# Attention and two MLPs on one core: layer 2 in two channel halves, weight checks by a second reading, one predicated copy a step

## The chip, the cores and the metric

The kernel runs on one NeuronCore of a Trainium2 chip. The time is the device time of one execution in microseconds (us); three runs were taken. [...]

## What is computed

Three layers in a row, all in float32. First attention with 2 batches, 8 heads, 768 positions and 64 channels a head, in which a query sees the 128 positions up to its own and the first few positions of the sequence (sinks). Then two MLPs on the 1536 tokens of 512 channels, each through 2048 hidden channels:

```
scores = where(is_sink | in_window, scale * q @ k.T, -1e9)
a = softmax(scores);  x = (a @ v), heads side by side      # 1536 x 512
h = x @ w_in1;  g = (a0 + a1 h + a2 h^2 + a3 h^3) / (1 + |b0||h| + |b1| h^2 + 1e-6);  x = g @ w_out1
h = max(x @ w_in2, 0);  out = (h * h) @ w_out2
```

The weights lie in memory as 8-byte words. The kernel turns them into float32 by integer operations on the two halves of each word, and a check that no weight is too small for that way is part of the program: a flag at the end of the kernel sends unusual inputs to a slow general path, which does not run here.

## The kernel before

**Precision.** Every matmul operand is split into a high and a low part (`xh`, `xl`; `gh`, `gl`; the two rows of a weight tile `w`), and three products are made of them, so each 128 x 128 x 512 block of a product costs three matmuls.

**Attention.** A block `u` is 128 queries of all heads; there are 12 blocks, six a batch, and each takes four steps `n` (two heads a step). In step `n` the program gives out, engine by engine and in the order of the code: ACT's exponentials of step `n-1` (`expo`, L371), PE's scores of step `n` into two PSUM banks `s` (L341), DVE's predicated copy and masked minimum of them (`s` L349, `ns` L354), PE's transposes of step `n-2` (L394), ACT's copies of the sink columns into `sk` (L383), POOL's two selects that make `ph` out of `pc` (L403, L407), PE's products with the values (`O` L431), and, once a block, the transpose of `sk` (L414), the products with the sinks' values (L438, L440), the scaling `x` (L443) and its transposes and split (L296, L212, L213). Queries and keys of the next block are split by ACT and POOL (`ql`, `kl`, L303). There are four banks `s`, so the scores of a step wait until DVE has read those of two steps before. PE also runs filler matmuls of zeros (L467), up to eight a step in the first twelve steps, three a step in the first block of a batch, and twelve at the end.

**Weights.** There are 64 weight tiles of 512 KB, 32 a layer. `w_load` has four of them on the way (tile `wr`). `w_step` takes a tile in four DVE instructions: a minimum of absolute values `wmin` (L164), then three integer operations (L171, L178, L183) that make the float32 tile `wx`. `w_fin` splits it by ACT and POOL into `w`. `w_until(due(k))` says how many of these instructions must have been given out by slot `k`: 13 tiles during attention, the other 19 of layer 1 until slot 30, ten of layer 2 until the end of layer 1, and the last 22 at two tiles a slot from there. In attention the function `extra` gives them out after each step but those with `n % 4 == 2`.

**Layers.** A slot `k` is one pass of 128 hidden channels `f` for a chunk `c` of 512 tokens: first the products with `w_in` into a bank `T` (function `g1`, 12 matmuls, L536), two slots later those with `w_out` into four banks `s` (`g2`, 12 matmuls, L612). In between lie the activation on ACT, DVE and POOL. Layer 1 has 48 slots: two halves `g` of the hidden channels, in each the three chunks, in each eight `f`. At the end of a chunk `finish` takes the four banks to SBUF: in the first half copies `part` (DVE L638 two, ACT L640 two), in the second half sums with them (DVE L635). Layer 2 has 48 slots too: three chunks of 16 `f`, and `finish` copies to `o` (DVE L644, ACT L646), from where SP sends it out. A bank `T` is free for `g1` of two slots on when DVE has read it for the last time (L577 in layer 1, L570 in layer 2), and PE waits for that. In slot `k` the order of the code is: split of the activation two slots back, `w_fin` twice, DVE's activation of `k-1` with `finish` ahead of it, `g1(k+1)`, ACT's activation of `k`, weight steps, `g2(k-2)`.

`verdict` makes the flag at slot 68, with one small matmul on PE and a reduction on DVE that waits for it.

Of the kernel before, what the change touches and what calls it, by code (L numbers as in the profile page):

```python
# [15 lines left out]
P = 128  # L16
# [3 lines left out]
WS = 4  # L20
# [6 lines left out]
LEAST = 2.0 ** -15 * 1.125  # L27


@with_exitstack  # L30
def kernel(
# [52 lines left out]
    hsum = cst.tile([P, NCH * NF], F32, name="hsum")  # L84

    wmin = cst.tile([P, 4 * NF], F32, name="wmin")

# [51 lines left out]
    parts = {}  # L139

    def w_load():
        m = wst["load"]
        if m >= len(wtiles):
            return
        wst["load"] += 1
        L, f, j = wtiles[m]
        src = ((w_in1, w_out1), (w_in2, w_out2))[L][j].bitcast(I32)
        r = wr.tile([P, DM, 2], I32, tag="wr", name="wr", bufs=NWR)
        if j == 0:
            nc.sync.dma_start(  # L150
                out=r.rearrange("p (c f) t -> p c (f t)", c=KD),
                in_=src[:, 2 * f * P:2 * (f + 1) * P].rearrange("(c p) f -> p c f", p=P),
            )
        else:
            nc.sync.dma_start(out=r.rearrange("p n t -> p (n t)"), in_=src[f * P:(f + 1) * P, :])
        wraw[m] = r

    def w_step():
        m, i = divmod(wst["int"], WS)
        wst["int"] += 1  # L160
        r = wraw[m]
        low, high = r[:, :, 0], r[:, :, 1]
        if i == 0:
            nc.vector.tensor_reduce(  # L164
                out=wmin[:, m:m + 1], in_=high.bitcast(F32), axis=AX.X, op=ALU.min, apply_absolute_value=True
            )
            return
        if i == 1:
# [6 lines left out]
            return  # L175
        x = wt[m]
        if i == 2:
# [3 lines left out]
        else:  # L181
            y = wx[m] = wr.tile([P, DM], I32, tag="wx", name="wx", bufs=2) if conv["psum"] else x
# [3 lines left out]
            del wraw[m], wt[m]  # L186
            w_load()

    def w_until(steps):
        while wst["int"] < min(steps, WS * len(wtiles)):  # L190
            if wst["int"] % WS == (WS - 1 if conv["psum"] else 1) and len(wx) == 2:
# [28 lines left out]
    def ps_s():  # L220
        return ps.tile([P, 512], F32, tag="S", name="s", bufs=4)
# [11 lines left out]
    def attention(ap, extra, ahead):  # L233
# [6 lines left out]
        ld, qs, vs, pr_t, pT, kps, ops, sk, sT, rs_t = {}, {}, {}, {}, {}, {}, {}, {}, {}, {}  # L240
# [90 lines left out]
        def scores(n):  # L331
# [3 lines left out]
            d = [ps_s() for _ in range(2)]  # L335
# [11 lines left out]

# [657 lines left out]
```

## Time and profile before

| | |
|---|---|
| three runs | 716.63, 718.15 (median), 720.15 us |
| span of the profiled execution, first to last instruction | 716.1 us |
| attention, until the first matmul of layer 1 | 152.7 us |
| matmuls of the two layers, to the last one's end | 557.4 us |
| PE busy | 689.8 us, 96% of the span |
| DVE, ACT, POOL busy | 447.8, 376.4, 355.7 us |
| TensorE's mean granted clock | 0.949 |

The profiler's span leaves out what lies around the program; the runs stand 0.5 to 4.1 us above it. PE's busy time is that of overlapping matmuls whose ends are modelled, so 96% says that PE is the engine to look at and not that nothing can be gained on it: what matters is at which clock it ran, and where it stood still.

### The profile page before, as it was taken

Reading aid. Unit: us, or ns where it says so; the run is one execution under the profiler, and the core shown is the slowest. Engines: PE = TensorE matmul, PEld = TensorE weight load, DVE = VectorE, ACT = ScalarE, POOL = GpSimd, SP = SyncE. Lnnn points to the kernel's source line nnn. Section 1 sums busy time; section 2 is a strip of 40 time slices with the busy share of each in tenths; the row PEclk is TensorE's granted clock in tenths of the full one; section 3 lists DMA queues with packets and bytes.
Section 4 is the critical chain, followed back from the end, with each engine's and each line's share of the span. In section 5 each row is a group of like instructions: output and inputs, shape, how many; then the busy total and the mean of one; then the engine's idle time right before and its main releaser. Section 6 shows DMA issues by size and latency. Waiting matters only on the chain.

```text
span 716.1 us, 9442 instructions
## 1 busy us (share of the span) xinstructions
PE 689.8 (96%) x3210; PEld 554.7 (77%) x3210; DVE 447.8 (63%) x942; ACT 376.4 (53%) x851; POOL 355.7 (50%) x341
## 2 busy tenths in 40 slices
PE   9999899997999999999999999899999999999996
PEld 6778788886877878878778788677787788878885
DVE  4899865548979979799797894999602211021111
ACT  4688654446868868778598692433322222222221
POOL 3788555324655646656486583776522222222221
PEclk9999755589999999999999999999999999999999
DMA  8556522101111212112021120555001000010001
GB/s 222 148 138 161 148 74 59 60 30 29 60 59 60 88 39 80 59 59 59 30 62 57 46 72 1 175 176 176 3 1 59 1 0 1 1 59 1 0 1 63
DMA packets 49016, 46.90 MB, mean 65 GB/s; under 512 B 14656, under 2 KB 43328, under 8 KB 48960
## 3 DMA queue, kind: packets, MB, share of 16 engines
q1 hardware_dynamic: 48960, 46.22, 21.8%
q8 instruction: 27, 0.44, 0.3%
q14 instruction: 29, 0.24, 0.1%
HBM read 43.06 MB, written 3.15 MB: 65 GB/s over the span
## 4 chain that ended last, share of the span: by engine, by line
PE 80%; DVE 15%; POOL 1%; ACT 1%; issue 1%; DMA 1%; SPq 0%; DVEq 0%; ACTq 0%
PE T L536 33%; PE s L612 31%; PE O L431 6%; PE s L341 4%; DVE wx L183 3%; PE T L394 2%; DVE O L178 2%; DVE wmin L164 2%; POOL w L204 1%; DVE O L171 1%; PE s L467 1%; DVE g L570 1%; DVE part L635 1%; PE U L296 1%; DVE t L577 1%
## 5 line engine op out<-in xcount | busy, mean ns | idle before, releaser
L536 PE MATMUL T<-xh,w 128*128 128x512 f32 x768 | 258.4, 398 | 14.8 <-DVE t L577 10.1
L536 PEld LDWEIGHTS T<-xh,w 128*128 128x128 f32 x768 | 145.0, 189 | 56.0 <-DVE t L577 13.4
L536 PE MATMUL T<-xl,w 128*128 128x512 f32 x384 | 151.0, 393 | 0.0
L595 POOL TENSOR_TENSOR gl<-g,gh 128x512 fp32r<-128x512 f32 x48 | 62.2, 1295 | 151.5 <-ACT gh L594 151.4
L612 PE MATMUL s<-gh,w 128*128 128x512 f32 x384 | 127.3, 392 | 0.0
L612 PE MATMUL s<-w,gh 128*128 128x512 f32 x384 | 119.7, 393 | 0.0
L570 DVE TENSOR_TENSOR g<-r,T 128x512 f32<-128x512 f32 x48 | 32.8, 686 | 129.6 <-ACT r L562 128.4
L204 POOL TENSOR_TENSOR w<-wx,w 128x512 fp32r<-128x512 f32 x64 | 83.7, 1308 | 22.5 <-ACT w L203 22.4
L558 POOL TENSOR_TENSOR t<-t,ah 128x512 f32<-128x512 f32 x48 | 62.2, 1297 | 63.4 <-ACT t L555 63.4
L595 POOL TENSOR_TENSOR gl<-t,gh 128x512 fp32r<-128x512 f32 x48 | 62.3, 1298 | 45.9 <-ACT gh L594 36.1
L612 PEld LDWEIGHTS s<-w,gh 128*128 128x128 f32 x384 | 72.1, 188 | 16.5
L612 PEld LDWEIGHTS s<-gh,w 128*128 128x128 f32 x384 | 72.2, 188 | 16.1
L536 PEld LDWEIGHTS T<-xl,w 128*128 128x128 f32 x384 | 72.7, 189 | 15.3
L612 PE MATMUL s<-w,gl 128*128 128x512 f32 x192 | 75.5, 393 | 0.0
L612 PE MATMUL s<-gl,w 128*128 128x512 f32 x192 | 75.2, 392 | 0.0
L562 ACT ACTIVATE r<-T 128x512 f32<-128x512 f32 x48 | 28.7, 598 | 78.3 <-PE T L536 77.3
L594 ACT CAST gh<-g 128x512 fp32r<-128x512 f32 x48 | 29.7, 619 | 67.9 <-PE s L612 64.6
L203 ACT CAST w<-wx 128x512 fp32r<-128x512 f32 x64 | 39.6, 618 | 44.8 <-DVE wx L183 44.7
L431 PE MATMUL O<-vr,ph 128*128 128x64 f32 x352 | 58.4, 322 | 0.7 <-POOL ph L407 0.7
L431 PEld LDWEIGHTS O<-vr,ph 128*128 128x128 f32 x352 | 58.0, 247 | 1.1 <-POOL ph L407 0.9
L594 ACT CAST gh<-t 128x512 fp32r<-128x512 f32 x48 | 29.8, 621 | 40.8 <-DVE t L587 30.2
L371 ACT ACTIVATE pe<-ns,nmax 128x136 f32<-128x136 f32 (+1 forms) x96 | 38.3, 401 | 14.4 <-DVE nmax L354 14.1
(133 smaller groups left out, 1097.8 us busy)
## 6 DMA issues: line engine op xcount, KB each, us to landing
wr<-in_w_in_dram SPq DMA_DIRECT2D x32, 512.0 KB, 3.7
wr<-in_w_out_dram SPq DMA_DIRECT2D x32, 512.0 KB, 3.6
qr<-in_q_dram SPq DMA_DIRECT2D x12, 256.0 KB, 4.2
kr<-in_k_dram SPq DMA_DIRECT2D x12, 256.0 KB, 4.6
vr<-in_v_dram SPq DMA_DIRECT2D x12, 256.0 KB, 4.8
out_dram<-o SPq DMA_DIRECT2D x12, 256.0 KB, 2.5
vsc<-in_v_dram SPq DMA_DIRECT2D x4, 16.0 KB
raw<-in_spans_dram SPq DMA_DIRECT2D x1, 2.0 KB
```

The source lines that it names most:

```text
L203: nc.scalar.copy(out=t[:, 0], in_=xf)
L204: nc.gpsimd.tensor_tensor(out=t[:, 1], in0=xf, in1=t[:, 0].bitcast(F32), op=ALU.subtract)
L341: nc.tensor.matmul(d[e][:, 0:w].rearrange("p (j n) -> p j n", n=bw), lhsT=ql[a][s, pr, :], rhs=kk[b][s, pr, slots, 0:bw], start=(a + b == ...
L371: nc.scalar.activation(out=t[:, e, 0:w], in_=ns[e][:, 0:w], func=ACTF.Exp, scale=-1.0, bias=nmax[:, ix:ix + 1], accum_out=rs[:, 2 * pr + e ...
L431: nc.tensor.matmul(o[:, h * D:(h + 1) * D], lhsT=pt[:, j, e], rhs=ld[u - 1 + j][2][:, h, :], start=(h == 0 and j == (i == 0)), stop=False, ...
L536: nc.tensor.matmul(h, lhsT=wi[a][:, kk * P:(kk + 1) * P], rhs=(xh, xl)[b][c][:, kk, :], start=(kk == 0 and a + b == 0), stop=(kk == KD - 1 ...
L558: nc.gpsimd.tensor_tensor(out=t, in0=t, in1=ah, op=ALU.mult)
L562: nc.scalar.activation(out=r, in_=h, func=ACTF.Relu)
L570: nc.vector.tensor_tensor(out=g, in0=st.pop(k), in1=h, op=ALU.mult)
L594: nc.scalar.copy(out=gh, in_=g)
L595: nc.gpsimd.tensor_tensor(out=gl, in0=g, in1=gh.bitcast(F32), op=ALU.subtract)
L612: nc.tensor.matmul(acc[L, g, c][m], lhsT=lh, rhs=rh, start=(f == f0 and a + b == 0), stop=(f == f1 and a == 1),)
```

## The change

In layer 2 the 48 slots are now ordered as in layer 1: the first eight `f` for all chunks, then the other eight. `finish` keeps the first half's sums in buffers that weights have left (`keep` holds six back for it), adds the second half to them on DVE and sends them out from there. The last 22 weight tiles are converted one a slot, over 22 slots.

`wmin` is no longer part of a conversion, but for those 22 tiles, where it comes last. The other 42 tiles are read from memory a second time in layer 2, and `wmin` of them is taken there, one tile a slot in the first 22 slots and then three in two slots. Two checks are new beside it: a maximum of the 16 tiles of `w_in1`, and one of `v` (six tiles of 512 KB, read again), in place of the sum `hsum` that ACT collected in layer 1. The flag is made at slot 93.

In attention the two banks of a step are one tile of two banks (`ps_s` gives pairs, in the layers too), the two predicated copies are one of 128 x 2 x 128, and the sink columns are copied once a block by POOL (new L417, 128 x 128 elements) instead of once a step by ACT.

```diff
-WS = 4
+WS = 3
...
+    LATE = 2 * NF + AHEAD
+    again = [("w", m) for m in range(LATE)] + [("v", i) for i in range(NV)]
+    jobs = [("c", m) for m in range(LATE)]
+    for m in range(LATE, 4 * NF):
+        jobs += [("c", m), again.pop(0)]
+    jobs += again
+    todo, ends, converted = [], [], []
+    for j, (kind, m) in enumerate(jobs):
+        todo += [(j, i) for i in range(WS + (m >= LATE) if kind == "c" else 1 + (kind == "w" and m < 2 * NF and m % 2 == 0))]
...
     def w_fin():
         m = wst["fin"]
-        if m >= wst["int"] // WS or not spare or int(spare[0][1:]) >= len(wpool):
+        if m not in wx or m in wt or len(spare) <= keep[0] or int(spare[0][1:]) >= len(wpool):
             return
...
     def ps_s():
-        return ps.tile([P, 512], F32, tag="S", name="s", bufs=4)
+        return ps.tile([P, 2, 512], F32, tag="S", name="s", bufs=2)
...
             if po is not None:
-
-                for e in range(2):
-                    nc.vector.copy_predicated(out=d[e][:, co:co + P], mask=tri, data=d[e][:, po:po + P])
+                nc.vector.copy_predicated(
+                    out=t[:, :, co:co + P], mask=tri.unsqueeze(1).to_broadcast([P, 2, P]), data=t[:, :, po:po + P]
+                )
...
         def sinks(n):
-            u, pr = divmod(n, NPR)
-            if u % NB == 0:
-                return
-            if pr == 0:
+            u = n // NPR
+            t = pe_t.pop(u)
+            if u % NB and n % NPR == NPR - 1:
                 sk[u] = ap.tile([P, 2, H, SK], F32, name="sk", bufs=2)
-            nc.scalar.copy(
-                out=sk[u][:, :, 2 * pr:2 * pr + 2], in_=pr_t[n][:, :, P:].unsqueeze(1).to_broadcast([P, 2, 2, SK])
-            )
+                nc.gpsimd.tensor_copy(
+                    sk[u], t[:, :, :, P:].rearrange("p r e s -> p (r e) s").unsqueeze(1).to_broadcast([P, 2, H, SK])
+                )
...
-    steps = [(0, g, c, f) for g in range(2) for c in range(NCH) for f in range(g * NF // 2, (g + 1) * NF // 2)]
-    steps += [(1, 0, c, f) for c in range(NCH) for f in range(NF)]
-    span = {(0, 0): (0, NF // 2 - 1), (0, 1): (NF // 2, NF - 1), (1, 0): (0, NF - 1)}
+    steps = [
+        (L, g, c, f) for L in range(2) for g in range(2) for c in range(NCH)
+        for f in range(g * NF // 2, (g + 1) * NF // 2)
+    ]
+    span = [(0, NF // 2 - 1), (NF // 2, NF - 1)]
...
             if f == f0:
-                acc[L, g, c] = [ps_s() for _ in range(4)]
+                acc[L, g, c] = [t[:, m] for t in [ps_s(), ps_s()] for m in range(2)]
...
+                if g == 0:
+                    (nc.scalar.copy if j else nc.vector.tensor_copy)(out=q, in_=src)
+                elif L == 0:
+                    nc.vector.tensor_tensor(out=q, in0=src, in1=q, op=ALU.add)
+                    late.append((c, j, m))
                 else:
-                    o = mp.tile([P, DM], F32, tag=("t", "t3")[m], name="o", bufs=2 + m)
-                    if j == 0:
-                        nc.vector.tensor_copy(o, src)
-                    else:
-                        nc.scalar.copy(out=o, in_=src)
+                    nc.vector.tensor_tensor(out=q, in0=src, in1=q, op=ALU.add)
                     r0 = c * CT + (2 * j + m) * P
-                    nc.sync.dma_start(out=out[r0:r0 + P, :], in_=o)
+                    nc.sync.dma_start(out=out[r0:r0 + P, :], in_=q)
...
-        return WS * (2 * NF + AHEAD + 2 * max(k - KL - 1, 0))
+        rest = 2 * NF - AHEAD
+        if k < KL + rest:
+            return ends[LATE + 2 * (k - KL) + 1]
+        return ends[min(LATE + 2 * rest + (3 * (k - KL - rest + 1)) // 2, len(jobs)) - 1]
```

Three places of the programs' order follow, all on DVE. The first is in attention, from the end of step 27 to the scores of step 28, the first step of the second block of batch 2; `x` and `xl1` belong to older blocks, `s` are the scores of step 28. Before:

```order
L443 TENSOR_TENSOR x_1268<-O_1151,rs_997 128x512
L213 TENSOR_TENSOR xl1_83<-T_1270,xh1_80 128x4x128
L164 TENSOR_REDUCE wmin_92<-wr_784 128x1
L171 TENSOR_SCALAR wx_1278<-wr_784 128x512
L178 SCALAR_TENSOR_TENSOR wx_1278<-wr_784,wx_1278 128x512
L349 COPY_PREDICATED s_1284<-tri_104,s_1284 128x128
L349 COPY_PREDICATED s_1285<-tri_104,s_1285 128x128
L354 ISA ns_1294,nmax_90<-s_1284,m_1_102 128x136
```

And after the change:

```order
L477 TENSOR_TENSOR x_1180<-O_1068,rs_929 128x512
L247 TENSOR_TENSOR xl1_83<-T_1182,xh1_80 128x4x128
L204 TENSOR_SCALAR wx_1189<-wr_733 128x512
L210 SCALAR_TENSOR_TENSOR wx_1189<-wr_733,wx_1189 128x512
L382 COPY_PREDICATED s_1194<-tri_105,s_1194 128x2x128
L389 ISA ns_1202,nmax_90<-s_1194,m_1_103 128x136
```

One reduction of 512 columns is gone from ahead of the scores of step 28, and one predicated copy; L204 and L210 are the old L171 and L178.

The second place is the end of the first chunk of layer 1. Before, the two copies read two tiles `s`:

```order
L587 SCALAR_TENSOR_TENSOR t3_2562<-t3_2562,na_87,U_2588 128x512
L638 COPY part_2633<-s_2252 128x512
L638 COPY part_2633<-s_2253 128x512
L575 TENSOR_TENSOR t3_2611<-t3_2611,T_2545 128x512
L171 TENSOR_SCALAR O_2637<-wr_2336 128x512
L577 SCALAR_TENSOR_TENSOR t3_2611<-t3_2611,na_87,T_2545 128x512
```

After, they read one, `s_2086`, and in the built program the first of them waits for the last matmul into the second bank of that tile:

```order
L623 SCALAR_TENSOR_TENSOR t3_2389<-t3_2389,na_87,U_2416 128x512
L670 COPY part_2461<-s_2086 128x512 x2
L611 TENSOR_TENSOR t3_2439<-t3_2439,T_2372 128x512
L210 SCALAR_TENSOR_TENSOR O_2414<-wr_2162,O_2414 128x512
L613 SCALAR_TENSOR_TENSOR t3_2439<-t3_2439,na_87,T_2372 128x512
```

The order has not moved; what the first copy waits for has, and one weight step still stands ahead of the instruction that frees the bank `T` (L577 before, L613 after).

The third place is the start of layer 2, from the last sum of layer 1 to the next activation `g2`. Before:

```order
L635 TENSOR_TENSOR part_3489<-s_4351,part_3489 128x512
L164 TENSOR_REDUCE wmin_92<-wr_4316 128x1
L171 TENSOR_SCALAR O_4726<-wr_4316 128x512
L178 SCALAR_TENSOR_TENSOR O_4726<-wr_4316,O_4726 128x512
L183 SCALAR_TENSOR_TENSOR wx_4729<-wr_4316,O_4726 128x512
L164 TENSOR_REDUCE wmin_92<-wr_4424 128x1
L171 TENSOR_SCALAR O_4734<-wr_4424 128x512
L178 SCALAR_TENSOR_TENSOR O_4734<-wr_4424,O_4734 128x512
L183 SCALAR_TENSOR_TENSOR wx_4737<-wr_4424,O_4734 128x512
L570 TENSOR_TENSOR g2_4767<-r_4721,T_4671 128x512
```

And after:

```order
L672 TENSOR_TENSOR part_3300<-s_4147,part_3300 128x512 x2
L204 TENSOR_SCALAR O_4547<-wr_4436 128x512
L210 SCALAR_TENSOR_TENSOR O_4547<-wr_4436,O_4547 128x512
L216 SCALAR_TENSOR_TENSOR wx_4550<-wr_4436,O_4547 128x512
L184 TENSOR_REDUCE wmin_91<-wr_4436 128x1
L184 TENSOR_REDUCE wmin_91<-wr_4456 128x1
L184 TENSOR_REDUCE wmax_92<-wr_4456 128x1
L606 TENSOR_TENSOR g2_4580<-r_4543,T_4479 128x512
```

Eight weight instructions between two activations have become six, and five in every second slot.

## Rows read from the trace of the kernel before

**Rows 1.** The page: PE's busy time; its granted clock in 40 slices of 17.9 us.

```profile
PE 689.8 (96%) x3210; PEld 554.7 (77%) x3210; DVE 447.8 (63%) x942; ACT 376.4 (53%) x851; POOL 355.7 (50%) x341
...
PEclk9999755589999999999999999999999999999999
```

**Rows 2.** Windows: stretch, length, busy us of each engine, PEclk, DMA share, GB/s.

```profile
60.00:80.00 20.00, 17.85 (x137) 14.08 (x137) 17.20 (x56) 12.96 (x48) 13.71 (x19) 1.00 0.65 172
80.00:100.00 20.00, 20.00 (x97) 16.82 (x97) 15.58 (x58) 12.37 (x50) 13.08 (x18) 0.50 0.32 93
...
140.00:160.00 20.00, 19.76 (x99) 16.57 (x99) 7.74 (x20) 9.10 (x27) 7.29 (x11) 0.80 0.14 45
```

**Rows 3.** The chain that ended last: start, length, what; two neighbouring attention blocks.

```profile
87.13 1.60 PE O L431 x8
...
102.42 1.60 PE O L431 x8
```

**Rows 4.** Timeline of PE in attention (start, length, instruction): blocks 4 and 5.

```profile
45.81 0.39 PE L341 MATMUL s<-kh,qh 64*128 64x272 f32 x2
...
55.06 0.40 PE L341 MATMUL s<-kh,qh 64*128 64x272 f32 x2
...
57.73 0.27 PE L414 MATMUL T<-ident,sk 128*128 128x128 f32 x1
```

**Rows 5.** Timeline, 76 to 80 us: the steps 27 to 30.

```profile
76.18 0.68 DVE L164 TENSOR_REDUCE wmin<-wr 128x1 f32<-128x512 f32 x1
...
76.77 0.42 DVE L171 TENSOR_SCALAR wx<-wr 128x512 int32<-128x512 int32 x1
...
77.17 1.27 POOL L303 TENSOR_TENSOR ql<-qr,qh 128x512 fp32r<-128x512 f32 x1 [4.13 <-ACT qh L302]
77.22 1.76 DVE L178 SCALAR_TENSOR_TENSOR wx<-wr,wx 128x512 int32<-128x512 int32 x1
78.91 0.48 DVE L349 COPY_PREDICATED s<-tri,s 128x128 f32<-128x128 int32 x2
...
79.74 0.68 DVE L183 SCALAR_TENSOR_TENSOR wx<-wr,wx 128x512 int32<-128x512 int32 x1
...
79.74 0.78 PE L341 MATMUL s<-kh,qh 64*128 64x272 f32 x2 [2.15 <-DVE nmax L354]
```

**Rows 6.** Timeline of POOL near 57 us; POOL's copies of 128 x 128 (groups).

```profile
57.30 0.40 POOL L407 TENSOR_SCALAR_AFFINE_SELECT ph<-pc 128x256 f32<-128x256 f32 x1
...
L317 POOL CAST kh<-kh 128x128 fp32r<-128x128 f32 x2 | 1.1, 525 | 0.0
...
L317 POOL CAST kl<-kl 128x128 fp32r<-128x128 f32 x2 | 0.6, 296 | 0.0
```

**Rows 7.** Timeline at the first chunk's end in layer 1.

```profile
212.31 1.38 DVE L638 COPY part<-s 128x512 f32<-128x512 f32 x2 [4.73 <-PE s L612]
...
215.60 0.50 PE L536 MATMUL T<-xh,w 128*128 128x512 f32 x1 [1.23 <-DVE t L577]
```

**Rows 8.** Layer 2: PE's timeline while weights are converted, then the chain without.

```profile
450.89 0.50 PE L536 MATMUL T<-xh,w 128*128 128x512 f32 x1 [1.41 <-DVE g L570]
456.93 0.50 PE L536 MATMUL T<-xh,w 128*128 128x512 f32 x1 [0.27 <-DVE g L570]
...
574.04 2.80 PE T L536 x12
...
607.40 2.80 PE T L536 x12
```

**Rows 9.** Timeline at the first chunk's end in layer 2, and the last copies.

```profile
536.95 1.46 DVE L644 COPY o<-s 128x512 f32<-128x512 f32 x2 [10.12 <-PE s L612]
...
538.62 0.40 PE L612 MATMUL s<-w,gl 128*128 128x512 f32 x1
539.05 0.50 PE L536 MATMUL T<-xh,w 128*128 128x512 f32 x1
...
709.49 1.28 ACT L646 COPY o<-s 128x512 f32<-128x512 f32 x2 [4.43 <-PE s L612]
```

More of the change, by code (lines that the diff above doesn't have):

```diff
@@ L139 @@
     parts = {}
+    keep = [0]
+    LATE = 2 * NF + AHEAD
[7 more added lines that the diff above has]
+        todo += [(j, i) for i in range(WS + (m >= LATE) if kind == "c" else 1 + (kind == "w" and m < 2 * NF and m % 2 == 0))]
+        ends.append(len(todo))
+        if kind == "c":
+            converted.append(len(todo))
@@ L158, in w_step, with extreme @@
+        wraw[j] = r
+    def extreme(dst, src, op):
+        nc.vector.tensor_reduce(out=dst, in_=src, axis=AX.X, op=op, apply_absolute_value=True)
     def w_step():
-        m, i = divmod(wst["int"], WS)
+        j, i = todo[wst["int"]]
         wst["int"] += 1
-        r = wraw[m]
+        kind, m = jobs[j]
+        r = wraw[j]
+        if wst["int"] == ends[j]:
+            del wraw[j]
         low, high = r[:, :, 0], r[:, :, 1]
[L163 to L166, printed above, removed]
-            return
@@ L185, in w_step @@
             )
-            del wraw[m], wt[m]
+        if wst["int"] == ends[j]:
             w_load()
     def w_until(steps):
-        while wst["int"] < min(steps, WS * len(wtiles)):
-            if wst["int"] % WS == (WS - 1 if conv["psum"] else 1) and len(wx) == 2:
+        while wst["int"] < min(steps, len(todo)):
+            j, i = todo[wst["int"]]
+            if jobs[j][0] == "c" and i == (WS - 1 if conv["psum"] else 0) and len(wx) == 2:
                 return
@@ L334, in scores @@
             w = bw if po is None else 2 * bw
-            d = [ps_s() for _ in range(2)]
+            t = ps_s()
+            d = [t[:, e] for e in range(2)]
             fill(d[0], DENSE[n] if n < len(DENSE) else DENSE_B if u % NB == 0 else 0)
@@ L660, in split_late @@
             if m == 1:
-                del parts[c, j]
-                spare.append(f"b{NW - 2 * (c + 1) + j}")
+                spare.append(parts.pop((c, j))[1])
+                if c == NCH - 1 and j == 1:
+                    keep[0] = 2 * NCH
         K = len(steps)
@@ L708, in verdict @@
         d = ps_t("U")
-        nc.tensor.matmul(d[0:2, 0:8], lhsT=ones, rhs=bad, start=True, stop=True)
+        nc.tensor.matmul(d[0:2, 0:9], lhsT=ones, rhs=bad, start=True, stop=True)
         n = sp.tile([1, 1], F32, tag="nbad", name="nbad")
-        nc.vector.tensor_reduce(out=n, in_=d[0:1, 0:8], axis=AX.X, op=ALU.add)
+        nc.vector.tensor_reduce(out=n, in_=d[0:1, 0:9], axis=AX.X, op=ALU.add)
         fl = cst.tile([1, 1], I32, name="fl")
```

117 lines of the change are left out of this document (62 added, 55 removed).

## Prediction

> **What bounds the kernel now.** The page comes first: PE is busy for 96% of the span, but its granted clock drops for some four slices early on [rows 1]. The windows give the place: the clock is at 1.00 up to 80 us and at 0.50 after it; the mean of 0.80 in the stretch from 140 to 160 says that 8 us of that one still ran at half speed, so the half clock lasts from about 80 to 148 us, 68 us in all [rows 2]. In it DVE is busy for 15.6 of 20 us where it had 17.2 in a stretch in which PE lost 2 us: at half clock PE alone sets the pace. The chain shows how fast that pace is: the same products come back 15.29 us later, one block of four steps [rows 3]. At full clock the timeline has a block at 9.25 us [rows 4]. So the half clock costs some 6 us a block, for about four and a half blocks. No other item of this profile is of that size.
>
> What stood ahead of the drop is in the timeline: PE waited 2.15 us for DVE before the scores of step 30, and the clock is at half when it goes on [rows 5]. The wait of 1.23 us at the end of a chunk in layer 1 [rows 7] left the clock at full, as the strip shows [rows 1].
>
> In the layers PE runs without a break except in three kinds of place: the ends of chunks [rows 7, 9], the entry into layer 2, and the ten steps after it, which take 6.04 us (456.93 - 450.89) where six later ones take 33.36, or 5.56 each [rows 8].
>
> **The change part by part.** *Attention, step 30.* DVE's order ahead of the scores of step 28 was wmin, L171, L178, two predicated copies; wmin goes. It took 0.59 us, start to start. L178 began at 77.22, just after POOL's ql at 77.17, and took 1.76 us where L183 alone takes 0.68 [rows 5]. Without wmin it stands at 76.18 + 0.45 = 76.63 and is done at about 77.3, with POOL's ql behind it or beside it. The copy and the minima, 0.83 us before (78.91 to 79.74) and some 0.06 less as one copy, then end near 78.1. PE stops at 77.59 as before, so its wait becomes 0.5 us: 1.6 us won, of which I take 1.5. The bounds of the single copy: no gain, if 256 elements cost what two times 128 did, and at most half of the pair's 0.48 us.
>
> [...]
>
> *Attention, the clock.* If PE waits only 0.5 us here, I expect the clock to stay up, and blocks 8 to 11, which have the shape of block 4, to run at its pace. The 68.3 us are 68.3 / 15.29 = 4.47 blocks. At 9.25 us and a new wait of 0.55 (next) they take 43.8: **-24.5 us**. Bounds: 27.0 with no new wait, 22.1 with twice that wait.
>
> *Attention, the sink columns.* They move from ACT to POOL, behind the two selects of the step before. The second select ends at 57.70 and POOL's copy of 128 x 128 takes 0.30 to 0.53 us [rows 6], so `sk` is there at 58.0 to 58.2, and PE asks for it at 57.73 (L414) [rows 4]: a new wait of 0.3 to 0.5 us a block, more where selects run late. I take 0.55. What is queued behind PE's wait is the rest of its step; behind POOL's copy, ql of the next block, which ACT and the selects already keep late. Four blocks ahead of 80 us have it: **+2.0**. At half clock PE would come later and not wait.
>
> wmin's other removals here and in layer 1 (0.68 us of DVE a tile, 42 tiles), and the ACT copies, are worth nothing beyond step 30: PE was running while they ran. If PE's cover went, each would give back its own length.
>
> *Layer 1, ends of chunks.* The first copy started at 212.31 and the second 0.69 later, when its bank was ready (1.38 for both) [rows 7]. Now both wait for the second bank, and the first costs its own 0.60 more; then come L611, a weight step and L613, which frees T for PE, as before. PE's wait grows from 1.23 to about 1.8 us. Five ends: **+3.0**. Below, nothing, if the copies were not on PE's way; above, 0.69 each, three matmuls' time.
>
> *Entry into layer 2.* The same 0.6, but of the eight weight instructions between two activations six are left, and the 1.41 us that PE waited for L570 [rows 8] go: **-0.8**.
>
> *Conversion.* A slot has 4 + 1 or 2 weight instructions and one activation, 7 at most, by 0.6 to 0.8 us (6.04 / 9 = 0.67 in the old steps): 4.7 us at most, under PE's 5.56. Ten steps by 0.48: **-4.8** [rows 8]. The second readings are two loads a slot, as many as before, for 22 slots instead of 11; they wait for buffers, and nobody on PE's way waits for them.
>
> *Layer 2, ends of chunks.* Before, PE's last matmul of the chunk started at 538.62 and g1 at 539.05, where 0.23 apart is the rule (5.56 / 24): a wait of 0.2 [rows 8], with a slower restart some 0.3 [rows 9]. There were two. Now there are five, and each has the 0.6 of the pair: 5 x 0.9 - 0.6 = **+3.9**. Below, +0.9 without the 0.6.
>
> *The end.* ACT copied the last two banks from 709.49 in 1.28 us, the first of them while PE still worked [rows 9]. Now DVE adds both after PE's last matmul: **+0.6**. The verdict moves to slot 93 with the same chain of PE, DVE and PE, at the same price.
>
> *Sum* against the span of 716.1: -1.5 - 24.5 + 2.0 + 3.0 - 0.8 - 4.8 + 3.9 + 0.6 = -22.1, a span of 694.0. The median of the runs is 2.05 above the span, so **696 us**.
>
> **The rivals.** *A: the clock falls where it fell.* For it: POOL's ql may start first, since ACT's cast ahead of it also moves up when ACT loses work; then L210 is held to where L178 ended, the predicated copy starts at 78.91 as before, and PE waits 2.1 us. Also, this trace shows one wait in attention with a drop behind it and no other of like length to compare. Against it: L210 has 0.54 us in hand, and both chains start from the same transposes of PE. Then -24.5 is gone, half of -1.5 stays, and the rest is +3.9: 716.1 + 3.2 + 2.05 = 721 us. This is also the case in which the change does nothing where the time is.
>
> *B: the clock stays at step 30 but falls in one of the blocks after it*, which this trace shows at half clock alone; DVE's collisions with POOL could line up once more. A block at half clock costs 15.3 - 9.8 = 5.5 us: one to three blocks give 701 to 713 us.
>
> *C, on the other side: the wait for `sk` on POOL brings the clock down earlier*, at step 17, where blocks have no fillers and a select held up by DVE, as L178 was by POOL, would add to the copy. From step 17 to 30 it is 13 steps, 3.25 blocks, more at half clock: 721 + 3.25 x 5.5 = 739 us. It decides as soon as that wait is as long as the one at step 30 was. Against it: POOL's copy is one short instruction, and the largest wait that I can build from the rows is under 1 us.
>
> **How the numbers follow.** The forecast has a chance of 0.58; its own range is 690 to 701, from the bounds of the clock term (-2.5, +2.4), the single copies of the ends of chunks (down to -6, of which I take half), and a second 0.55 us a block. A has 0.24, B 0.10, C 0.08. Three runs of one kernel differ by 3.5 us, so about 0.5% (714.6 to 721.7) is what can be told from no change. The forecast and B are faster: 0.68. A lies at the edge of that band, two thirds of it inside: same 0.16, slower 0.08 + 0.08 = 0.16. A range of 8 in 10 takes in the forecast, B, and A to 722: **689 to 722**.
>
> **What would show it.** Right: PEclk at full strength in all slices of attention but the last, blocks of 9 to 10 us between 80 and 120 us, the first matmul of layer 1 near 128 us instead of 152.7. In the row of L210 of step 27, a duration near 0.7 us. L414 waiting for POOL's L417 by half a microsecond. At the ends of chunks PE waits of 1.8 us in layer 1 and near 0.9 in layer 2, five times each; steps of 5.5 us from the start of layer 2. Wrong: a stretch at 0.50 with L210 at 1.7 us is A; a stretch that begins later is B, earlier is C. If the steps of layer 2 stay at 6 us, loads or DVE hold them, and the conversion term was wrong; if the waits at ends of chunks stay at 1.23, the pair of banks costs nothing and the time is 3 to 6 us lower.

## The result and the profile after

The changed kernel took 730.38, 753.57, 726.99 and 753.06 us, beside 716.63 to 720.15 us (median 718.1) for the kernel before. The comparison takes 727.0 and 730.4: a ratio of 1.0143, 95% interval 1.0107 to 1.0179, slower by 1.4%; the two runs at 753 us are slower by 4.9%. I had forecast 696, with a range of 689 to 722. The runs of one kernel come in groups some 17 to 31 us apart, and the mean granted clock of a run goes with its group (here 0.94 and 0.90), so below I give groups and not medians.

The profiled run is that of 730.38 us, with a span of 728.7. In the rows PE is TensorE and PEld its weight loads, DVE is VectorE, ACT ScalarE, POOL GpSimd and SP SyncE; PEclk is TensorE's granted clock as a share of full speed. Every stretch of the clock records of this profile and of that before stands at 1.00 or at 0.50 (half clock), and other values are means. The page of the run, PE's busy time and clock, beside [rows 1]:

```profile
PE 696.0 (96%) x3210; PEld 559.7 (77%) x3210; DVE 473.8 (65%) x938; ACT 369.0 (51%) x763; POOL 357.8 (49%) x351
...
PEclk9999855588999999999999999999999999999999
```

The slices look as before. The windows (columns as in [rows 2]) show where the clock fell, and what the strip is too coarse for:

```profile
60.00:80.00 20.00, 19.18 (x149) 15.09 (x149) 14.64 (x54) 13.34 (x49) 15.11 (x21) 1.00 0.71 192
80.00:86.00 6.00, 3.62 (x31) 2.79 (x32) 5.68 (x16) 3.42 (x15) 3.87 (x4) 1.00 0.78 208
86.00:88.00 2.00, 1.10 (x10) 0.74 (x8) 1.86 (x7) 2.00 (x8) 1.07 (x3) 0.72 0.21 32
88.00:140.00 52.00, 52.00 (x245) 43.59 (x245) 28.88 (x102) 24.61 (x90) 28.12 (x43) 0.50 0.21 57
140.00:160.00 20.00, 20.00 (x92) 16.85 (x93) 6.68 (x21) 7.50 (x20) 6.35 (x12) 0.71 0.16 52
...
217.00:220.00 3.00, 1.17 (x5) 0.82 (x5) 3.00 (x6) 2.71 (x5) 0.25 (x1) 1.00 0.00 0
220.00:223.40 3.40, 3.40 (x10) 2.63 (x9) 3.33 (x6) 2.00 (x4) 1.95 (x2) 0.50 0.52 154
223.40:226.00 2.60, 2.60 (x12) 2.13 (x12) 2.49 (x5) 2.54 (x5) 2.12 (x3) 1.00 0.00 0
```

In attention the clock falls 7 us later than before (0.72 in 86 to 88 puts it at 86.9) and stays down almost as long: 65 us for 68. Ahead of the fall, from 80 to 86 us, PE works for 3.62 of 6 us. In layer 1 a stretch of 3.4 us at half clock stands behind the end of a chunk, which the kernel before does not have. The windows of the kernel before at its first chunk's end, where PE waits until 215.60 [rows 7]:

```profile
214.00:217.00 3.00, 1.77 (x8) 1.19 (x7) 3.00 (x6) 2.86 (x6) 0.49 (x1) 1.00 0.00 0
217.00:220.00 3.00, 3.00 (x15) 2.48 (x14) 2.96 (x6) 1.34 (x4) 1.29 (x2) 1.00 0.45 134
```

Timeline at steps 27 to 30, which answers to [rows 5]; L204, L210, L382 and L376 are L171, L178, L349 and L341 of before:

```profile
77.71 0.42 DVE L204 TENSOR_SCALAR wx<-wr 128x512 int32<-128x512 int32 x1
...
78.16 0.69 DVE L210 SCALAR_TENSOR_TENSOR wx<-wr,wx 128x512 int32<-128x512 int32 x1
...
78.70 1.28 POOL L337 TENSOR_TENSOR ql<-qr,qh 128x512 fp32r<-128x512 f32 x1 [4.49 <-ACT qh L336]
78.77 0.42 DVE L382 COPY_PREDICATED s<-tri,s 128x256 f32<-128x256 int32 x1
...
79.90 0.39 PE L376 MATMUL s<-kh,qh 64*128 64x272 f32 x2 [0.78 <-DVE nmax L389]
```

L210 is ahead of ql and takes 0.69 us, as forecast; PE's wait is 0.78 us for 2.15. Two steps later the same thing happens to other instructions (L313 makes vm, the sink values of the second half; L238 is POOL's part of a weight):

```profile
81.39 1.29 POOL L337 TENSOR_TENSOR kl<-kr,kh 128x512 fp32r<-128x512 f32 x1 [1.42 <-ACT kh L336]
81.45 1.77 DVE L313 TENSOR_TENSOR vm<-bd,vsc 128x512 f32<-128x512 f32 x1
...
82.65 1.71 POOL L238 TENSOR_TENSOR w<-wx,w 128x512 fp32r<-128x512 f32 x1
...
83.15 1.49 DVE L204 TENSOR_SCALAR wx<-wr 128x512 int32<-128x512 int32 x1
...
84.56 0.42 DVE L382 COPY_PREDICATED s<-tri,s 128x256 f32<-128x256 int32 x1
...
85.80 0.40 PE L376 MATMUL s<-kh,qh 64*128 64x272 f32 x2 [1.95 <-DVE rs L485]
```

L313 starts 0.06 us behind kl and L204 0.50 behind w; they take 1.77 and 1.49 us, where L313 takes 0.69 at 21.55 us, 0.32 ahead of kl, and L204 0.42 at 77.71 us, with POOL idle. The copy is late by that, and PE waits 1.95 us. (The last row names L485; it starts while the minima of L389 end, and those are what PE needs.)

The first chunk's end in layer 1, beside [rows 7]:

```profile
215.86 1.29 DVE L670 COPY part<-s 128x512 f32<-128x512 f32 x2 [5.56 <-PE s L648]
...
217.06 0.68 DVE L611 TENSOR_TENSOR t<-t,T 128x512 f32<-128x512 f32 x1
...
218.26 0.74 DVE L613 SCALAR_TENSOR_TENSOR t<-t,na,T 128x512 f32<-128x512 f32 x1
...
219.05 0.50 PE L573 MATMUL T<-xh,w 128*128 128x512 f32 x1 [1.83 <-DVE t L613]
```

Both copies of the pair run back to back behind the second bank. PE waits 1.83 us (1.82 to 1.86 at all five ends).

To split the span I take PE's first product of the third step of layer 1, that of layer 2, and the last product. Timeline of PE, before:

```profile
159.47 0.50 PE L536 MATMUL T<-xh,w 128*128 128x512 f32 x1 [0.24 <-DVE t L577]
...
427.19 0.40 PE L536 MATMUL T<-xh,w 128*128 128x512 f32 x1
...
709.71 0.40 PE L612 MATMUL s<-w,gl 128*128 128x512 f32 x1
```

The same after, with two of the entries and ends in layer 2, beside [rows 8, 9], and the last additions:

```profile
161.59 0.50 PE L573 MATMUL T<-xh,w 128*128 128x512 f32 x1 [0.16 <-DVE t L613]
...
440.54 0.40 PE L573 MATMUL T<-xh,w 128*128 128x512 f32 x1
...
457.68 0.50 PE L573 MATMUL T<-xh,w 128*128 128x512 f32 x1 [0.61 <-DVE g L606]
...
503.16 0.50 PE L573 MATMUL T<-xh,w 128*128 128x512 f32 x1 [0.58 <-DVE g L606]
...
720.23 2.65 DVE L675 TENSOR_TENSOR part<-s,part 128x512 f32<-128x512 f32 x4 [8.07 <-PE s L648]
...
721.17 0.39 PE L648 MATMUL s<-w,gl 128*128 128x512 f32 x1
```

| us | up to step 3 of layer 1 | layer 1 | layer 2 | rest | span |
|---|---|---|---|---|---|
| before | 159.5 | 267.7 | 282.9 | 6.0 | 716.1 |
| after | 161.6 | 279.0 | 281.0 | 7.1 | 728.7 |
| difference | +2.1 | +11.2 | -1.9 | +1.1 | +12.6 |
| forecast | -24.0 | +3.0 | -1.7 | +0.6 | -22.1 |

So two terms failed: the clock in attention, by 26 us, and the chunk ends of layer 1, by 8. My theory for the second: the pair of banks lengthens PE's wait, and the longer wait brings the clock down. For the first: either one held-up instruction does it, now at another place, or PE does so little in these blocks without fillers that any of them can lose the clock, and the pair makes it worse.

### The profile page after: what moved, and what is told of

Its sections match the earlier page's. It is cut to its first block, busy times and chain, and to the rows that moved or that the text cites. A ratio compares the mean times of both kernels' runs of the same rounds, so it can differ in the third digit from the quotient of the medians.

```text
span 728.7 us, 9431 instructions
## 1 busy us (share of the span) xinstructions
PE 696.0 (96%) x3210; PEld 559.7 (77%) x3210; DVE 473.8 (65%) x938; ACT 369.0 (51%) x763; POOL 357.8 (49%) x351
## 4 chain that ended last, share of the span: by engine, by line
PE 86%; DVE 7%; POOL 2%; issue 2%; ACT 1%; DMA 1%; SPq 0%; DVEq 0%; POOLq 0%
PE T L573 38%; PE s L648 34%; PE O L465 5%; PE s L376 3%; PE T L428 2%; PE s L501 1%; DVE part L670 1%; POOL ph L441 1%; DVE t L613 1%; PE U L330 1%; POOL ph L437 1%; DVE t L611 1%; DVE g L606 1%; DMA kr<-in_k_dram 1%; PE O L474 1%
## 5 line engine op out<-in xcount | busy, mean ns | idle before, releaser
L573 PE MATMUL T<-xh,w 128*128 128x512 f32 x768 | 263.2, 404 | 17.2 <-DVE t L613 12.6
L573 PEld LDWEIGHTS T<-xh,w 128*128 128x128 f32 x768 | 148.8, 194 | 56.8 <-DVE t L613 15.1
L573 PE MATMUL T<-xl,w 128*128 128x512 f32 x384 | 155.2, 404 | 0.0
L631 POOL TENSOR_TENSOR gl<-g,gh 128x512 fp32r<-128x512 f32 x48 | 62.1, 1294 | 168.6 <-ACT gh L630 168.6
L573 PEld LDWEIGHTS T<-xl,w 128*128 128x128 f32 x384 | 74.4, 194 | 16.3
L238 POOL TENSOR_TENSOR w<-wx,w 128x512 fp32r<-128x512 f32 x64 | 84.5, 1320 | 2.6 <-ACT w L237 2.6
L598 ACT ACTIVATE r<-T 128x512 f32<-128x512 f32 x48 | 28.8, 599 | 86.9 <-PE T L573 86.9
```

Source lines behind the costliest of these rows:

```text
L238: nc.gpsimd.tensor_tensor(out=t[:, 1], in0=xf, in1=t[:, 0].bitcast(F32), op=ALU.subtract)
L573: nc.tensor.matmul(h, lhsT=wi[a][:, kk * P:(kk + 1) * P], rhs=(xh, xl)[b][c][:, kk, :], start=(kk == 0 and a + b == 0), stop=(kk == KD - 1 ...
L598: nc.scalar.activation(out=r, in_=h, func=ACTF.Relu)
L631: nc.gpsimd.tensor_tensor(out=gl, in0=g, in1=gh.bitcast(F32), op=ALU.subtract)
```

## The experiments

In the tables "kept" counts the runs in which the clock stayed up through attention, by the run's mean clock (0.98 and more; 0.97 and more in kernels that still have the five stretches of layer 1), so a fall of a few microseconds does not count against a run. Of the kernel before 46 runs were made beside these kernels: 39 at 716.6 to 720.2 us with a clock of 0.94 to 0.95, and 7 at 693.2 to 694.0 with 0.99. The kernel before itself keeps the clock now and then, and is then 25 us faster (medians 693.8 and 718.9).

### The pair of banks

e1_banks takes the pairs out of the changed kernel, e2_pair puts them into the kernel before. The edit of e1_banks (e2_pair is its reverse):

```diff
-        return ps.tile([P, 2, 512], F32, tag="S", name="s", bufs=2)
+        return ps.tile([P, 512], F32, tag="S", name="s", bufs=4)
...
-                nc.vector.copy_predicated(
-                    out=t[:, :, co:co + P], mask=tri.unsqueeze(1).to_broadcast([P, 2, P]), data=t[:, :, po:po + P]
-                )
+                for e in range(2):
+                    nc.vector.copy_predicated(out=d[e][:, co:co + P], mask=tri, data=d[e][:, po:po + P])
...
-                acc[L, g, c] = [t[:, m] for t in [ps_s(), ps_s()] for m in range(2)]
+                acc[L, g, c] = [ps_s() for _ in range(4)]
```

> The changed kernel with single banks again (four tiles of one bank, two predicated copies a step); all else of the change stays. Theory: the pair makes the first copy at the end of a chunk wait for the second bank; that lengthens PE's wait in layer 1 from 1.23 to 1.83 us, and the longer wait is followed by 3.4 us at half clock, which costs another 1.7 us. So here: five waits of 1.2 us, clock at full behind them, 5 x (0.6 + 1.7) = 11.5 us less in layer 1, and about 0.3 less at each of five ends in layer 2: 727 to 730 becomes 714 to 718. Rival 1: the wait goes back but the half clock behind it stays, since it hangs on another part of the change: 723 to 727. Rival 2: the wait stays at 1.8 us, since it is another engine that ends it: no change.

> The kernel before with the pair of banks alone (one predicated copy a step, and pairs for the sums of layers 1 and 2). Theory: the same five waits of 1.8 us, each with 3.4 us at half clock behind it, so 5 x 2.3 = 11.5 us more in layer 1, and some 0.6 in layer 2: 718 becomes 729 to 731; attention about the same (wait at step 30 above 1.5 us, clock lost there). Rival: the drop of the clock belongs to another part of the change, and only the waits grow: 721 to 722.

e1_banks: 711.9 to 712.7 us in four runs, layer 1 back at 268.2 us. Its timeline at the same chunk's end:

```profile
211.70 1.39 DVE L668 COPY part<-s 128x512 f32<-128x512 f32 x2 [4.86 <-PE s L646]
...
213.01 0.68 DVE L609 TENSOR_TENSOR t<-t,T 128x512 f32<-128x512 f32 x1
...
214.21 0.74 DVE L611 SCALAR_TENSOR_TENSOR t<-t,na,T 128x512 f32<-128x512 f32 x1
...
215.00 0.50 PE L571 MATMUL T<-xh,w 128*128 128x512 f32 x1 [1.23 <-DVE t L611]
```

The first copy starts 0.7 us earlier against PE's last product, three of its products, and the wait is that of [rows 7]. No half clock follows:

```profile
200.00:400.00 200.00, 193.78 (x835) 156.02 (x834) 162.82 (x249) 149.25 (x239) 122.42 (x96) 1.00 0.19 57
```

e2_pair: 731.9 and 733.9 us, and 756.2 and 756.6; five waits of 1.82 to 1.86, 3.4 us at half clock behind each, layer 1 at 278.3 us. In layer 1 both went as the theory said (e1_banks came out some 2 us below its range, the two faster runs of e2_pair 1 to 3 us above theirs): the pair alone costs layer 1 10.6 us (278.3 - 267.7), 3 of them as waits (5 x 0.6) and the rest at half clock. Without it the change is 6.8 us faster than the kernel before (medians 712.3 and 719.2 of the runs beside each other that lose the clock in attention).

In attention e2_pair did not go as the theory said. Its profiled run has three stretches at half clock there, of 3.4, 6.8 and 54.6 us, the first from 70.3 us on, with the clock at full between them; and its two runs at 756 us are in a group that the kernel before has in none of 46 runs. The pair changes attention too, then, with the sink columns still on ACT.

### The order at the chunk ends

e4_order leaves the pairs and writes the copies behind the products that free T; e5_both does so with single banks.

```diff
             h = hq.pop(k)
-            finish(0)
...
                 gq["f", k] = g
+                finish(0)
                 finish(1)
...
             nc.vector.scalar_tensor_tensor(out=t3, in0=t3, scalar=na[:, 1:2], in1=h, op0=ALU.add, op1=ALU.mult)
+            finish(0)
             fill()
```

> The changed kernel with the copies at the end of a chunk (L670, L675) written behind L613 in layer 1 and behind L606 in layer 2, where they were ahead of them; the pairs stay. Theory: PE's next products wait for L613 alone, and L613 for the copies ahead of it in DVE's order. So the five waits of 1.83 us in layer 1 go, and the 3.4 us at half clock behind each: 5 x (1.8 + 1.7) = 17.5 us less, and six waits of 0.6 us in layer 2, 3.6 less: 727 to 730 becomes 706 to 710. Rival: the sums' banks then come free later, and PE waits for them before the first product into them instead, some 1.2 us an end with the clock at full: 713 to 716.

> The changed kernel with single banks and with the copies written behind L613 and L606, both. Single banks alone gave 712.3 with five waits of 1.23 us in layer 1 and the clock at full behind them. Theory: the five waits go as they did with the other order alone: 5 x 1.23 = 6.2 us less, 706 to 707, where the clock falls in attention at the same place (87 us). Rival: with single banks nothing is left of PE's wait but the copies themselves, which then hold the banks: 709 to 712.

e4_order: 706.0 and 706.2 us (723.7 and 727.8 at a lower clock); no wait over 0.5 us is left at any chunk's end, and layer 1 takes 260.5 us. e5_both: 701.2 to 704.6 in six runs, layer 1 260.4 and layer 2 275.7; that is some 4 us below the 706 to 707 expected, and layer 1 alone gave 7.8 us (268.2 - 260.4) where five waits of 1.23 make 6.2. DVE's order made PE wait, not the copies: DVE sat idle for 5.56 us ahead of them in the row of L670 above, and L611 and L613, all that PE needs, fit in there.

### The clock in attention

e14_no_minima does the part on which my clock term rested; e3_pause and e13_vm move single instructions of DVE out of the way.

e14_no_minima, on the kernel before (the columns of `wmin` are set to 1.0 at the start instead):

```diff
+        if i == 0 and not conv["psum"]:
+            return
         if i == 0:
```

e3_pause, on the changed kernel, ahead of the call that takes due_a:

```diff
+                if 28 <= n < 34:
+                    due_a = (WS * NA * 23) // (NU * NPR - 4)
```

e13_vm, on e5_both:

```diff
-            if u < NU and u % NB == 1 and pr == 1:
+            if u < NU and u % NB == 0 and pr == 3:
                 sink_values(u // NB)
-            if u < NU and u % NB == 1 and pr == 3:
+            if u < NU and u % NB == 1 and pr == 1:
                 sink_split(u // NB)
```

> The kernel before without the minima of the weights that are converted in attention (13 instructions of DVE, wmin; this part of the check of the weights is left out). It does that part of the change alone on which the forecast's clock term rests. Theory as forecast: PE's wait of 2.15 us before the scores of step 30 falls to about 0.5, the clock stays up to the end of attention: 694 to 698 in all runs. Theory B: the wait at step 30 goes, but the clock falls in one of the next blocks all the same: 712 to 720 in most runs, the fall a few us later than 79.8.

> The changed kernel without weight instructions on DVE in steps 28 to 33 of attention; they follow in the steps behind, the same number in all. Theory: the clock fell at 86.9 us because of the wait of 1.95 us before the scores of step 32, which comes from L313 and L204 on DVE, each held up beside an instruction of POOL. Without L204 in their way the copy of step 32 comes 1.4 us earlier, the wait is about 0.5 us, and the clock stays up until the next wait of this kind. If none comes, 64.9 us at half clock, 4.24 blocks of 15.29, become blocks of 9.8: 23 us less, 704 to 708. If one comes in the blocks behind, 6 us less for each block that is won. Rival: the clock falls at 80 to 88 us whatever these waits are: 727 to 730 again.

> The kernel of e5_both (single banks, later copies, no fillers) with DVE's product of the sink values (L313 of the changed kernel) and its split two steps earlier, in the block that has fillers, so that it no longer runs beside POOL's kl of block 8. In e5_both the clock fell at 83.5 us in all runs, behind three waits of under half a microsecond. Theory A: it is this product, 1.8 us of DVE in the place of 0.7, that thins PE's work between 80 and 87 us; then the clock stays up there, and the runs are at 679 to 684 (702.7 less 23), or 684 to 702 if a later block loses it. Theory B: without fillers, PE does so little in these blocks that any block can lose the clock, and moving one product only shifts the place: 700 to 704 in most runs.

e14_no_minima: 689.4 to 691.3 us in five runs, 714.9 to 715.3 in three. The profile is of one of the three; its timeline at step 30:

```profile
76.01 0.69 DVE L181 SCALAR_TENSOR_TENSOR wx<-wr,wx 128x512 int32<-128x512 int32 x1
76.54 1.28 POOL L306 TENSOR_TENSOR ql<-qr,qh 128x512 fp32r<-128x512 f32 x1 [4.48 <-ACT qh L305]
...
77.45 0.58 PE L344 MATMUL s<-kh,qh 64*128 64x272 f32 x2 [0.49 <-DVE nmax L357]
```

The wait fell to 0.49 us, the 0.5 of the forecast, and PE has no other over 0.35 us near it. The clock is at half from 80.4 us on all the same:

```profile
80.00:100.00 20.00, 19.77 (x94) 16.44 (x94) 14.11 (x51) 11.62 (x49) 12.54 (x18) 0.51 0.31 90
```

So the long wait is not needed for the fall; without it, the clock is kept more often (5 runs of 8; the kernel before kept it in 7 of 46, and in none of the 11 made beside these 8). Neither theory's numbers hold for all runs.

e13_vm is the counterpart: vm was out of the way, but L210 now came 0.07 us behind ql, and the old wait was back:

```profile
77.40 1.26 POOL L337 TENSOR_TENSOR ql<-qr,qh 128x512 fp32r<-128x512 f32 x1 [4.44 <-ACT qh L336]
77.47 1.74 DVE L210 SCALAR_TENSOR_TENSOR wx<-wr,wx 128x512 int32<-128x512 int32 x1
...
79.97 0.58 PE L375 MATMUL s<-kh,qh 64*128 64x272 f32 x2 [2.14 <-DVE nmax L387]
```

Four runs at 703.7 to 704.7 us, three at 678.2 to 679.7. Neither theory's numbers hold for all; that the place shifts speaks for B. (83.5 us is the place in e5_both's profiled run; the places in its other five, with mean clocks of 0.944 to 0.953, were not traced.)

e3_pause missed: 737.7 to 738.1 us three times, 754.4 and 755.6. Up to step 28 it is the changed kernel, and it lost the clock before that, as the windows of its profile show:

```profile
20.00:39.00 19.00, 18.10 (x136) 13.52 (x136) 16.17 (x53) 12.36 (x47) 13.17 (x20) 1.00 0.40 106
39.00:60.00 21.00, 21.00 (x104) 17.48 (x103) 13.90 (x49) 10.96 (x39) 14.14 (x20) 0.51 0.49 127
```

What it was to tell about step 32 stays open. It shows something else: ahead of the fall, at 37.4 us, PE waits 0.90 us, and the profile of the changed kernel, the same program up to there, has the same wait of 0.90 us at 37.2 us and keeps the clock for 49 us more. That the runs of the changed kernel at 753 us, with the same mean clock of 0.90, lost it near 39 us too is likely but was not traced.

### Fillers

These kernels put filler products on zeros ahead of the transposes of attention, 42 by the trace (the expectations say 40):

```diff
             if n >= NP - 2:
                 fill(d, DENSE_E)
+            elif n >= 10:
+                fill(d, 2 if n < 14 or 26 <= n < 32 else (n + 2) // 4 % NB > 0)
```

e12_few has only the doubled ones, 20.

> The kernel of e5_both, with filler products of 128 x 512 ahead of the transposes of attention: two in the steps of blocks 3 and 7 and the first two of block 8, one in the others that had none, 40 in all, on zeros and overwritten. Theory: the clock falls in attention in a stretch in which PE did little, so products that PE makes while it would wait for DVE or ACT keep it up, and 62 us at half clock (some 23 us of time) are given back, less at most 40 x 0.21 = 8.5 us for the fillers: 683 to 692 where e5_both has 706, and all runs alike. Rival: the fillers lengthen each step, DVE starts later, the waits grow with them and the clock falls as before: 706 to 715.

> The kernel before with the same 40 filler products and nothing of the change. Theory: the clock stays up through attention in it too, which measures the term of the forecast by itself: 718 becomes 694 to 702 (24.5 us less the fillers' 0 to 8.5). Rival: the drop at 80 us comes from the wait of 2.15 us whatever stands around it: 718 to 726.

> The changed kernel with the same 40 filler products and nothing else. Theory: what the change costs with the clock held in attention is the five drops at the ends of chunks alone: 703 to 712, which is 5 to 11 us above the kernel before with fillers, less some 5.6 that layer 2 gains. Rival: the pair lengthens waits in attention too, the clock falls there in spite of the fillers, and the runs stay apart as those of the changed kernel did: 727 or more.

> The changed kernel with pairs of banks kept, with the copies behind L613 and L606, and with the 40 fillers: it differs from the kernel of e6_fill by the pairs alone. Theory: the pair has a price in attention too, since the one copy starts only when both banks are full; PE then waits longer in single steps, and the clock falls in some runs in spite of the fillers: part of the runs near 685, part 10 us and more above. Rival: the pair's whole price lay at the ends of chunks, and the other order has removed it: 683 to 686 in all runs.

> The kernel of e6_fill with 20 fillers only, those of blocks 3 and 7 and the first two of block 8, where the clock has been seen to fall. Theory: it falls only where DVE and POOL get into each other's way, so that these are enough, and the others cost up to 20 x 0.21 = 4 us: 679 to 683. Rival: other blocks lose it as soon as they have no fillers: 690 to 706 in part of the runs.

The 0.21 us a filler that the expectations add up is shown by no run: in the profile of the kernel before, eight fillers in a row start at 8.50 us and the product behind them at 10.53, 0.25 each.

| kernel | pair | fillers | us | kept |
|---|---|---|---|---|
| before | no | no | 716.6-720.2; 693.2-694.0 | 7 of 46 |
| after | yes | no | 727.0-730.4; 753.1-753.6 | 0 of 4 |
| e7_before_fill | no | 42 | 696.5-698.5 | 6 of 6 |
| e6_fill | no | 42 | 682.9-684.6 | 4 of 4 |
| e8_after_fill | yes | 42 | 706.9-712.1; 733.3-738.7 | 4 of 6 |
| e9_pair_fill | yes | 42 | 686.2-687.0; 717.5-718.0 | 2 of 6 |
| e12_few | no | 20 | 679.6; 704.8-707.4 | 1 of 6 |

e7_before_fill adds fillers and nothing else: 718 becomes 697.7, so the half clock of the kernel before is worth at least 20 us; its own runs that keep the clock say 24.4 (718.1 - 693.7). Held against those runs, the 42 fillers cost 4.0 us (697.7 - 693.7), 0.10 each. e6_fill holds the clock where e5_both loses it; two windows of its profile:

```profile
80.00:100.00 20.00, 18.27 (x137) 14.49 (x137) 18.20 (x65) 13.55 (x51) 15.14 (x20) 1.00 0.34 93
100.00:120.00 20.00, 19.97 (x156) 16.27 (x155) 18.38 (x66) 13.95 (x52) 15.70 (x25) 1.00 0.34 93
```

The clock is at 1.00 in both, where [rows 2] has 0.50; those rows themselves have 137 instructions of PE at 1.00 and 97 at 0.50, so the 137 and 156 here are no measure of what the fillers add. All runs of the four kernels with 42 fillers and single banks keep the clock, 20 of 20 (e7_before_fill, e6_fill, and e10_act_sinks and e11_before_order below). The fillers also move all that follows in time. That it is PE's added work that holds the clock, and not the shift, is argued and not shown; e12_few moves it too and keeps the clock once in six runs.

e9_pair_fill differs from e6_fill by the pairs alone, and loses the clock in four runs of six: the pair has a price in attention too. e8_after_fill is the changed kernel with the clock held in attention in four runs of six, at 707 to 712 us. It kept its five half-clock stretches in layer 1, and in the profiled run (711.8 us) the clock was at half for 7 us more from 89 us on. In e12_few the clock fell at 87.7 us behind a wait of 1.10 us; e6_fill waits 1.10 us near the same place (before 87.1 us) and kept the clock, and e9_pair_fill waits 1.51 us there (before 87.5 us) and kept it too. The length of a wait in attention does not decide by itself. What PE did around it may; these traces do not show it place by place.

### Small terms

> The kernel of e6_fill with the sink columns copied by ACT in each step again, as before the change. The forecast gave their move to POOL a cost of 2.0 us, at full clock. If that holds: 681 to 682. Rival: with fillers ahead of the transposes PE does not come to L448 before POOL is done, and ACT's four copies a block cost as much as POOL's one: 683 to 685.

> The kernel before with the 40 fillers and with its copies at the ends of chunks behind the products of the activation. Theory: five waits of 1.23 us go: 697.7 becomes 690 to 692, and the kernel of e6_fill (683.4) stands 6 to 8 us below it by the ten steps of layer 2 and the entry into it. Rival: most of what e6_fill has won was the order, and the change's conversion in layer 2 is worth 2 us or less: 684 to 686.

e10_act_sinks calls `sinks` in every step again, with ACT's copy of the kernel before: 682.4 to 683.8 us, median 683.1, against 682.9 to 684.6, median 683.4. With fillers, the move is worth nothing that can be told. e11_before_order is the kernel before with e4_order's order and the 42 fillers: 687.3 to 689.1 us, median 688.0, between the two theories. So 4.5 us of e6_fill are the change's own, less than I expected: layer 2 is 6.1 us shorter (281.8 to 275.7), attention 1.3 longer and the end 0.5.

Of the kernels whose runs all agree, e6_fill (683.4 us) and e10_act_sinks are the best. e6_fill is 4.9% under the median of the kernel before beside it (718.4), and at 0.9855 (interval 0.9831 to 0.9878) of the two of those runs that kept the clock.

## Why the prediction was wrong

**The clock, -24.5.** The term came out as +2.1 for all of attention, where -24.0 was forecast. The failed step is "If PE waits only 0.5 us here, I expect the clock to stay up". The wait shrank nearly as worked out (0.78 us in the changed kernel; 0.49 in e14_no_minima, where it can be seen by itself), and the clock did hold at step 30. But it fell 7 us later, 1.1 us behind the end of a wait of 1.95 us, which is rival B's mechanism, "DVE's collisions with POOL could line up once more", to which I had given 0.10, and priced at one to three blocks; 65 us are 4.2. I took one wait with a drop behind it for the cause. e14_no_minima shows the drop without the wait, e7_before_fill and e6_fill show it gone with products put ahead of the transposes, and the kernel before keeps the clock in 7 of 46 runs with nothing changed. What exactly brings the clock down stays open.

The size was nearly right, in part by luck. The runs of the kernel before that keep the clock and those that lose it are 25.1 us apart. In that kernel nothing waits for `sk` on POOL, so the figure of mine to set beside this is the bound without a new wait, 27.0. A block at full clock then takes some 9.7 us (an estimate: (68.3 - 25.1) / 4.47) and not the 9.25 that I read from one pair of blocks.

**Attention, step 30, -1.5.** I held the other removals of `wmin` to be worth nothing. The runs of e14_no_minima that keep the clock are some 4 us below those of the kernel before that do (medians 689.8 and 693.8), where step 30 alone was to give 1.5; with the clock held the others are worth something too.

**Layer 1, ends of chunks, +3.0.** The waits are those of the forecast, 1.83 us for 1.8. The term is 11.2 because 3.4 us at half clock follow each. I had read in [rows 7] that a wait of 1.23 us leaves the clock at full, and priced 1.8 us as if that held there too.

**A place that I passed over.** I wrote that PE runs in the layers without a break except in three kinds of place, and took from the strip of [rows 1] that a wait of 1.23 us leaves the clock at full. That is so (the windows above show it), but the strip is too coarse to show it: a slice is 17.9 us long, and 3.4 us at half clock leave its digit at 9. The trace of the kernel before has a fourth place, at the start of layer 1, and there the clock falls at the end of a wait:

```profile
168.72 0.79 PE L536 MATMUL T<-xh,w 128*128 128x512 f32 x1 [3.24 <-DVE t L577]
...
170.00:172.00 2.00, 2.00 (x6) 1.52 (x6) 1.97 (x4) 0.93 (x3) 1.02 (x1) 0.51 0.00 0
```

The clock is at half for 3.4 us from 168.6 us on. All 16 profiled runs wait 3.24 or 3.25 us here, with 3.4 or 6.8 us at half clock; e6_fill still does.

**One copy a step.** I bounded it between nothing and a gain of half. The instruction gains the 0.06 us that I took (L382 0.42, L349 0.48), but the pair that it needs loses the clock in attention more often (e9_pair_fill against e6_fill). A cost on this side was not in my bounds.

**Sink columns, +2.0.** Two waits of PE for POOL before step 32, of 0.40 and 0.59 us, where I had four of 0.5. One of them:

```profile
49.51 0.29 POOL L417 COPY sk<-pe 128x128 f32<-128x128 f32 x1
...
49.85 0.33 PE L448 MATMUL T<-ident,sk 128*128 128x128 f32 x1 [0.59 <-POOL sk L417]
```

**Layer 2 and the entry, -1.7.** Measured -1.9: steps of layer 2 without a chunk's end or the verdict take 5.4 to 5.7 us from the first one on, where the ten had taken 6.04, and at the ends PE waits 0.57 to 0.62 us where I took 0.9 in all. The end of the program is +1.1 for +0.6: of the four additions in a row on DVE (2.65 us) two lie behind PE's last product, 0.7 us more than ACT's copy before, as worked out; the rest is behind the last addition, and its cause was not looked into.

**The rivals.** A (721) had the right size of the loss in attention and the wrong place. C, an earlier fall, is what e3_pause's profile shows, but at 39 us and not from `sk` at step 17. Runs above 750 us came only from kernels with the pair (the changed kernel, e2_pair, e3_pause); none of the 17 runs of e1_banks, e5_both and e13_vm, which copy `sk` on POOL without the pair, is above 713 us. So the early fall goes with the pair and not with `sk`.

At the places shown, DVE's time went with the order of the starts: L210 took 0.69 us where it started 0.54 ahead of ql (after), and 1.74 where it started 0.07 behind (e13_vm); L204, 0.50 behind w, took 1.49 us for the 0.42 beside an idle POOL (after). I had reckoned with this for the one pair of instructions that collided before, not for those that the earlier start would bring together.

## What to carry to other kernels

A stall that stood ahead of a clock drop in one trace is a suspect, not a cause: look at several runs' mean clock first, and ask what PE does in the whole stretch. Removing one stall moves all that follows, so check what the next instructions run into; with single banks, 42 products on zeros held the clock in all runs (20 of 20), and no rearrangement did (e5_both none of 6, e13_vm 3 of 7). Where one tile covered two banks, its first reader waited for the last writer (0.7 us later at the first chunk's end, after beside e1_banks); and what frees the buffer that PE waits for goes ahead of copies on that engine, which here was worth more (9.7 us, e7_before_fill to e11_before_order) than the change without the pair (4.5 us, e11_before_order to e6_fill).

## What was not expected of the hardware

In layer 1, 20 waits of 1.82 to 1.86 us stand in four traces (after, e2_pair, e3_pause, e8_after_fill); behind 19 of them the clock is at half for 3.4 us. Behind the 15 of 1.23 to 1.27 us in three traces (before, e1_banks, e7_before_fill) it never is. In attention it fell in e5_both at 83.5 us with no wait above half a microsecond within 20 us; the waits ahead of that place, and the window behind it:

```profile
78.60 0.58 PE L375 MATMUL s<-kh,qh 64*128 64x272 f32 x2 [0.49 <-DVE nmax L387]
83.22 0.69 PE L375 MATMUL s<-kh,qh 64*128 64x272 f32 x2 [0.45 <-DVE nmax L387]
...
83.50:87.00 3.50, 3.06 (x16) 2.44 (x15) 3.46 (x11) 3.33 (x13) 3.18 (x7) 0.51 0.58 142
```

The same program keeps the clock in one run and loses it in the next (the kernel before keeps it in 7 of 46, e13_vm in 3 of 7, e14_no_minima in 5 of 8); what differs between two such runs no trace here shows. In the changed kernel the half clock begins 0.2 to 1.1 us behind the ends of its five waits in layer 1 (waits that end at 219.05, 266.66, 314.50, 362.72 and 410.99 us, half clock from 220.00, 267.79, 315.57, 363.36 and 411.15), at no fixed distance. What exactly keeps the clock up stays open.
